# Transposing DMAs for one more chunk's mixer and mlp rows, with a new schedule table

## The chip, the cores and the metric

The kernel runs on one core of a Trainium2 chip. The core has five engines, each with its own queue of instructions: PE (TensorE, matmuls and, beside them, the loading of weights), ACT (ScalarE), DVE (VectorE), POOL (GpSimd) and SP (SyncE, which here only issues DMAs). They meet through semaphores. The metric is the device time of one execution in microseconds (us); less is better.

## The reference

Two layers, each an attention and a mixer with an mlp, over 2048 rows of 512 elements in bf16. All four residual additions take place on the same x.

```python
def _A_ref(x, wq, wk, wv, wo):              # 32 query heads of 16, one key and value head
    q = (x @ wq).reshape(B, S, H, Dh).transpose(0, 2, 1, 3)
    k = x @ wk
    v = x @ wv
    p = softmax(einsum("bhqd,bkd->bhqk", q, k) * Dh ** -0.5)
    return einsum("bhqk,bkd->bhqd", p, v).transpose(0, 2, 1, 3).reshape(B, S, H * Dh) @ wo

def _B_ref(x, w1, w2, w3, w4):
    h = gelu(layernorm(x) @ w1)
    # four quarters of the columns, shifted by +1, -1, +2, -2 rows, zeros at the ends
    hs = concatenate([g0, g1, g2, g3], axis=-1) @ w2
    x1 = x + hs
    return x1 + gelu(layernorm(x1) @ w3) @ w4    # w3: 512 x 1792

for _ in range(2):
    x = x + _A_ref(layernorm(x), A_wq, A_wk, A_wv, A_wo)
    x = x + _B_ref(layernorm(x), B_w1, B_w2, B_w3, B_w4)
```

The attention has 2 x 32 x 2048 x 2048 scores, each of which needs an exponential.

## The kernel before

**Tiles and chunks.** The 2048 rows are 16 tiles of 128. A chunk is the group of query tiles that attention handles together: four chunks of four tiles in the first layer; in the second four, four, four, two and two (`CHUNKS`). So "the second layer's third chunk" is tiles 8 to 11, in the code `la == 1` and `c == 2`.

**Attention.** For each chunk, eight blocks of four heads, each over 16 blocks of keys. PE makes scores into PSUM (`qk`, line 1256). A half of a block's scores is then turned into exponentials in one of two ways. ACT does it with its exp function, 128 x 1024 at a time (`declare_unit`, line 1299, tile EA). Or DVE makes an approximation from integer arithmetic on the bits of a bf16 number, 128 x 512 at a time (`declare_pair`, line 1319, tile J), and two shifted copies of J follow (`shift_op`, line 1356), on POOL or DVE, whichever the planner finds freer; a shift takes one or two rows of 1024. PE multiplies both kinds by the values (`declare_pv`, line 1411; with EA and VP, or with J and VD) into an accumulator, which DVE copies out (line 1460).

**Normalising.** An accumulator goes to DRAM and back by SP (lines 1467 and 1469), its sums too (1551 to 1561). For the last blocks PE does it (lines 1528, 1579, 1594).

**After a chunk's attention** (`chunk_end`). Per tile the output projection (`outproj`, lines 815 and 1724), then the mixer (`mixer_in`, `mix`) and the mlp (`mlp`, `mlp_out`). Line 815 is that of the helper `dot`, which issues most matmuls in groups of four. `mixer_in` takes statistics (950, 952, 972, 970 and others), normalises into Y (987), and POOL normalises once more into ZR (1738). `mlp` normalises Y into ZR on DVE (987). ZR has four slots, and tile `tb` uses slot `tb % 4`, in both. The rows must then be transposed into ZT, so that PE can contract over the columns; this happens in one of two ways, which is what the change is about:

- `across`: PE transposes against an identity matrix, 16 small matmuls a tile (line 1034), into PSUM, and DVE copies two tiles at a time from there to ZT (line 1043).
- `ship`: SP issues one transposing DMA a tile, from ZR to ZT (line 1049); PE, PSUM and DVE have no part in it.

`shipped` (line 1052) chooses by layer and chunk. For the mlp the chunk is that of the group's first tile. The mlp of a chunk works on the tiles that have all their neighbours (`ripe`), so it runs one tile behind: in the second layer tiles 0 to 2, 3 to 6, 7 to 10, then 11 and 12, then 13 to 15.

W1's products go to GP (line 1768, or by ACT with gelu at 1764 in the last chunk), gelu runs over them (1777), two columns at the edges are copied between chunks by POOL (1788, 1790), and `mix` multiplies by W2. The mlp's 14 column blocks are cast to G (line 1864), gelu runs over a tile of G at a time (line 1879), and `mlp_out` multiplies by W4 and adds to X (1898). W3 comes in seven loads through three slots (RING). A change of function on ACT between exp and gelu needs a table load, which the profile lists as ACT_TABLE_LOAD.

**What sets the order.** `Plan` is a list scheduler that runs when the kernel is built. It keeps a heap of ready operations per engine, and its own model of durations, and writes out a fixed order for each engine. It decides there too which halves of the scores go to DVE (`assign`), and which engine shifts; and it puts in filler matmuls (`filler`, IDENT by NIL) where it expects PE to be idle too long. So the number of exponentials on ACT is an outcome of the planning. `TEMPER` is a string with one digit per 5 us of planned time (`STRETCH`); `temper` takes the digit as an index into `MOODS`, sets of limits by which the planner chooses. Any change of it, or of one operation, can move all later ones.

Of the kernel before, what the change touches and what calls it, by code (L numbers as in the profile page):

```python
# [661 lines left out]
class Kernel:  # L662
# [54 lines left out]
    )  # L717
    TEMPER = (
        "2280110c0c4d0a5404a77cda3cec04ccc043cb888a8e7685c67a47d737a46d1da4c7c8087cb1e28da695756a5c"
        "cc5401146a1d88c663f0b1a828a71d6771b4777604c30177000144c8400603ca66525013c2ad97e6e0064640a8"  # L720
        "bc0140560764745d734a7cdaddd3a20b49aa7716ba6d7772a777054b4aac3cb0217daf153ba686b0b548c6cc20"
        "1d522133002012000"
    )

    def __init__(self, nc, ins, out):
# [325 lines left out]

    def shipped(self, kind, la, c):
        last = c == len(self.CHUNKS[la]) - 1
        return c<=1

    def ln_in(self, la, tiles, prio=None):

# [882 lines left out]
```

## Time and profile before

| | |
|---|---|
| median of 3 runs | 1440.35 us (1439.69 to 1441.27) |
| the profiled execution's own time | 1442.68 us |
| its span, from first to last instruction | 1440.8 us |
| mean granted TensorE clock | 0.996 |
| transposing DMAs into ZT | 38, of 46 in all |
| their issue on SP | 1.25 us median |
| issue to landing | 2.4 / 2.5 / 4.4 us (least, median, most) |
| casts from PSUM to ZT (line 1043) | 16, of 0.41 to 0.69 us |
| first exponential begins, last ends | 13.5 us, 1376.6 us |

The profile is of one execution, and its times run from the start of the span. Of a group of instructions it gives the line in the kernel, the engine, the tiles written and read, the shapes and the count, then the busy time, the mean time of one in ns, and the engine's idle time before them with what ended it. PE's busy time is modelled, as matmuls are pipelined. The chain that ended last is followed back from the last instruction, step by step, to what released each.

### The profile page before, as it was taken

The page shows a single profiled execution, that of the slowest core. Times are in us where ns is not written, and L with a number is a line of the kernel's source. Part 1 is how long each engine was busy: PE and PEld are TensorE (multiplying, and loading weights), DVE is VectorE, ACT ScalarE, POOL GpSimd, SP SyncE. Part 2 cuts the span into 40 slices and gives each one's busy share as a digit, 9 for nine tenths or more (in the row PEclk, how much of TensorE's full clock was granted, in tenths as well). Part 3 has the DMA queues.
Part 4 walks back from the last instruction along what each step waited for, and adds up shares of the span by engine and source line. Part 5 has one row for each costly group of instructions (what it writes and reads, how often), then busy time and mean ns, then how long its engine had stood idle before and what let it go on. Part 6 is the DMA issues. An engine that isn't in the chain of part 4 may idle for free.

```text
span 1440.8 us, 61689 instructions
## 1 busy us (share of the span) xinstructions
PE 1415.1 (98%) x27972; PEld 624.6 (43%) x27972; DVE 1311.7 (91%) x2348; ACT 1374.1 (95%) x1463; POOL 1143.0 (79%) x807
## 2 busy tenths in 40 slices
PE   8999999999999999999999999999999999999999
PEld 4344334443433444444344434434434335545575
DVE  8999999999999998998988899999999999978863
ACT  7999999999999999999989999999999999999952
POOL 2888999888889888897855498888889888878831
PEclk9999999999999999999999999999999999999999
DMA  5200121101221011211011011320021111113122
GB/s 156 38 13 17 32 64 43 45 19 37 54 45 49 18 28 45 54 46 36 20 54 32 17 32 29 83 60 23 18 61 39 49 35 46 33 48 78 41 76 59
DMA packets 124335, 63.97 MB, mean 44 GB/s; under 512 B 43945, under 2 KB 124073, under 8 KB 124073
## 3 DMA queue, kind: packets, MB, share of 16 engines
q1 hardware_dynamic: 124072, 60.03, 16.4%
q8 instruction: 219, 3.59, 1.0%
q14 instruction: 44, 0.35, 0.1%
HBM read 40.14 MB, written 10.29 MB: 35 GB/s over the span
## 4 chain that ended last, share of the span: by engine, by line
ACT 63%; PE 18%; DVE 9%; POOL 7%; DMA 1%; issue 1%; SPq 0%; POOLq 0%
ACT EA L1299 59%; PE PB L815 7%; DVE J L1319 6%; POOL J L1356 5%; PE PB L1256 5%; PE PB L1411 5%; ACT G L1879 2%; DVE J L1356 1%; ACT GP L1777 1%; ACT L1299 1%; DVE ST L950 1%; POOL SM L970 1%; ACT L1777 1%; POOL ZR L1738 0%; DMA ad_dram<-ACCF 0%
## 5 line engine op out<-in xcount | busy, mean ns | idle before, releaser
L1299 ACT ACTIVATE EA<-PB 128x1024 bf16<-128x1024 f32 x1381 | 1271.3, 1145 | 16.0 <-PE PB L1256 15.2
L1356 POOL TENSOR_SCALAR J<-J 128x2048 uint16<-128x2048 uint16 (+1 forms) x538 | 992.0, 1844 | 192.4 <-DVE J L1319 83.9
L1319 DVE TENSOR_SCALAR J<-PB 128x512 uint16<-128x512 f32 x1334 | 848.2, 680 | 48.7 <-PE PB L1256 44.0
L1256 PE MATMUL PB<-QT,KT 32*128 32x512 bf16 (+1 forms) x4608 | 590.2, 361 | 8.6 <-ACT EA L1299 3.3
L1411 PE MATMUL PB<-J,VD 128*32 128x256 bf16 (+1 forms) x8964 | 421.1, 265 | 3.8 <-POOL J L1356 1.9
L1411 PE MATMUL PB<-EA,VP 128*32 128x256 bf16 (+1 forms) x6228 | 335.4, 265 | 4.0 <-ACT EA L1299 1.1
L1256 PEld LDWEIGHTS PB<-QT,KT 32*128 32x128 bf16 x4608 | 160.5, 91 | 382.6 <-ACT EA L1299 287.0
L1411 PEld LDWEIGHTS PB<-J,VD 128*32 128x32 bf16 x8964 | 188.8, 96 | 164.5 <-issue 111.0
L1411 PEld LDWEIGHTS PB<-EA,VP 128*32 128x32 bf16 x6228 | 143.9, 96 | 128.6 <-issue 106.6
L815 PE MATMUL PB<-ZT,RING 128*32 128x512 bf16 (+2 forms) x2112 | 128.5, 339 | 0.1
L1356 DVE TENSOR_SCALAR J<-J 128x2048 uint16<-128x2048 uint16 (+1 forms) x165 | 118.5, 719 | 10.4 <-POOL J L1356 8.1
L815 PE MATMUL PB<-W,G 128*32 128x512 bf16 x1624 | 106.2, 381 | 1.0 <-ACT G L1879 1.0
L1864 DVE CAST G<-PB 128x512 bf16<-128x512 f32 (+2 forms) x126 | 71.7, 577 | 12.0 <-PE PB L815 11.6
L970 POOL TENSOR_TENSOR SM<-SM,MH 128x2 f32<-128x2 f32 (+1 forms) x69 | 52.7, 765 | 21.8 <-DVE SM L972 11.2
L815 PEld LDWEIGHTS PB<-W,G 128*32 128x32 bf16 x1624 | 41.4, 96 | 38.1 <-issue 17.2
L815 PEld LDWEIGHTS PB<-ZT,RING 128*32 128x32 bf16 x2112 | 46.0, 96 | 27.0 <-issue 22.0
L1879 ACT ACTIVATE G<-G 128x1792 bf16<-128x1792 bf16 x29 | 46.9, 1683 | 9.8 <-DVE G L1864 9.7
L1898 DVE TENSOR_TENSOR X<-PB,X 128x512 bf16<-128x512 f32 x32 | 21.9, 686 | 30.5 <-PE PB L815 30.0
L1842 POOL TENSOR_TENSOR X<-Y,X 128x512 bf16<-128x512 bf16 x32 | 38.9, 1225 | 11.4 <-DVE Y L1820 8.6
L950 DVE BATCH_NORM_STATS2 ST<-X 128x6 f32<-128x512 bf16 x64 | 43.1, 683 | 2.4 <-DMA X<-in_A_x_dram 1.9
L1460 DVE CAST ACCF<-PB 128x512 bf16<-128x512 f32 (+1 forms) x65 | 40.0, 616 | 0.8 <-PE PB L1411 0.5
L815 PE MATMUL PB<-ZT,W 128*32 128x512 bf16 (+1 forms) x576 | 38.9, 358 | 0.3 <-issue 0.3
(110 smaller groups left out, 682.0 us busy)
## 6 DMA issues: line engine op xcount, KB each, us to landing
RING<-in_B_w_dram SPq DMA_DIRECT2D x66, 256.0 KB, 2.9
ad_dram<-ACCF SPq DMA_DIRECT2D x54, 128.0 KB, 1.8
WO<-in_A_wo_dram SPq DMA_DIRECT2D x9, 512.0 KB, 3.8
WO<-in_B_w_dram SPq DMA_DIRECT2D x9, 512.0 KB, 4.7
OT<-ad_dram SPq DMA_DIRECT2D x108, 32.0 KB
OZ<-rd_dram SPq DMA_DIRECT2D x21, 128.0 KB
X<-in_A_x_dram SPq DMA_DIRECT2D x8, 256.0 KB, 4.8
QT<-QS SPq DMA_DIRECT2D x32, 64.0 KB, 2.4
```

The costliest lines, as they stand in the source:

```text
L815: ins = e.matmul(self.PB[32 * g:32 * g + 32, bank, 0:n], lhsT=lhsT[:, 32 * g:32 * g + 32], rhs=rhs, start=start, stop=stop, tile_position= ...
L950: op("DVE", lambda e, tb=tb: e.bn_stats(self.ST6[:, tb, :], src(tb)), reads=[tagf(tb)], writes=[("ST", tb)], dur=0.606, prio=prio)
L970: op("POOL", lambda e: e.tensor_tensor(out=out, in0=src, in1=self.MH[:, 0, a:b], op=ALU.pow), reads=tags + [("MH",)], writes=tg(r), dur=0. ...
L1256: ins = e.matmul(self.PB[:, bank, j * n:(j + 1) * n], lhsT=self.KT[32 * h:32 * h + 32, la, (kb + j) * 128:(kb + j + 1) * 128], rhs=self.QT ...
L1299: o = q.feeds = op("ACT", lambda e: e.activation(self.EA[:, ea, :, :], self.PB[:, L.bank[0]:L.bank[0] + 2, :], ACTF.Exp, scale=0.25), writ ...
L1319: o = op("DVE", lambda e, i=i, L=L: e.tensor_scalar(out=self.J[:, 3 * s, i * 512:(i + 1) * 512], in0=self.PB[:, L.bank, :], scalar1=128 * ...
L1356: o = self.pl.op(eng, lambda e: e.tensor_scalar(out=self.J[:, d, :], in0=self.J[:, f, :], scalar1=float(self.STEP), scalar2=1.0, op0=ALU.a ...
L1411: ins = e.matmul(self.PB[32 * x:32 * x + 32, A.bank, p * hw:p * hw + hw], lhsT=v[:, la, kb + j, :], rhs=ap[:, i, j * w + u * hw:j * w + u ...
L1460: self.last_copy = op("DVE", lambda e: e.tensor_copy(acc, self.PB[:, A.bank, 0:n]), writes=[ac] + am, dur=t_ps(n), prio=0, side=False, give=A)
L1842: op("POOL", lambda e, tb=tb: e.tensor_tensor(out=self.X[:, tb, :], in0=self.Y[:, tb % 6, :], in1=self.X[:, tb, :], op=ALU.add), reads=[(" ...
L1864: op("DVE", lambda e, f=f, L=L: e.tensor_copy(self.G2[:, f, 0:n], self.PB[:, L.bank, 0:n]), writes=[L] + [(x, f, i) for x in ("G2", "GE") ...
L1879: self.pl.op("ACT", lambda e, i=i: e.activation(self.G2[:, :, i * 128:(i + 1) * 128], self.G2[:, :, i * 128:(i + 1) * 128], ACTF.Gelu_appr ...
```

## The change

`shipped` returns true also for the third chunk of the second layer. That takes in the mixer's rows of tiles 8 to 11, and the mlp's rows of tiles 11 and 12, whose group begins in that chunk: six tiles. (The mlp's group 7 to 10 begins in the second chunk, and its rows were transposed by DMA before too.) The rows for the queries, keys and values (`ln_in`) pass a layer of 0 to the function, so nothing changes for them. `TEMPER` is replaced by another string of the same length, 287 digits, 250 of which differ. As the planner sees other operations and other limits, the whole order is new from the first microseconds on.

```diff
     TEMPER = (
-        "2280110c0c4d0a5404a77cda3cec04ccc043cb888a8e7685c67a47d737a46d1da4c7c8087cb1e28da695756a5c"
-        "cc5401146a1d88c663f0b1a828a71d6771b4777604c30177000144c8400603ca66525013c2ad97e6e0064640a8"
-        "bc0140560764745d734a7cdaddd3a20b49aa7716ba6d7772a777054b4aac3cb0217daf153ba686b0b548c6cc20"
-        "1d522133002012000"
+        "028606a8707aa0a4a077377c7cac7ae13ac54718897680e0973c0a03a3e7e776fcc0220817730020c6cca60782"
+        "775e7d7e7cacd88876a516237797007a4a75c2c7c57521686ec0c005c0020101725002060c7dc72040e07c21b1"
+        "8146c0055672aaaa739ea77bcdcbc228747c710108554c776c0cde367ac00a8866607027567605621a20517472"
+        "0bd80203022000203"
     )
...
     def shipped(self, kind, la, c):
         last = c == len(self.CHUNKS[la]) - 1
-        return c<=1
+        return c<=1 or la and c<=2
```

## The prediction

> **What bounds the kernel now.** I read the page's busy shares, its chain that ended last, and its costliest groups, in that order.
>
> ```profile
> PE 1415.1 (98%) x27972; PEld 624.6 (43%) x27972; DVE 1311.7 (91%) x2348; ACT 1374.1 (95%) x1463; POOL 1143.0 (79%) x807
> ...
> ACT 63%; PE 18%; DVE 9%; POOL 7%; DMA 1%; issue 1%; SPq 0%; POOLq 0%
> ...
> L1299 ACT ACTIVATE EA<-PB 128x1024 bf16<-128x1024 f32 x1381 | 1271.3, 1145 | 16.0 <-PE PB L1256 15.2
> ```
>
> ACT carries the chain: 1381 exponentials at 1271.3/1381 = 0.921 us each, idle only 16.0 us before them. PE's 98% is modelled matmul ends and says little. So I asked the timeline of ACT where its idle time lies, and the windows for the clock in the two other gaps.
>
> ```profile
> 728.04 17.52 ACT L1299 ACTIVATE EA<-PB 128x1024 bf16<-128x1024 f32 x19
> 751.02 9.27 ACT L1299 ACTIVATE EA<-PB 128x1024 bf16<-128x1024 f32 x10 [5.46 <-PE PB L1256]
> 760.31 1.28 ACT L1879 ACT_TABLE_LOAD   x1
> 761.61 4.87 ACT L1879 ACTIVATE G<-G 128x1792 bf16<-128x1792 bf16 x3
> ...
> 1376.59 1.28 ACT L1777 ACT_TABLE_LOAD   x1
> 1378.82 1.06 ACT L1777 ACTIVATE GP<-GP 128x1024 bf16<-128x1024 bf16 x1 [0.94 <-DVE G L1864]
> ...
> 415.00:420.00 5.00, 5.00 (x67) 1.61 (x64) 4.20 (x8) 3.53 (x4) 4.83 (x3) 0.67 0.25 30
> ...
> 1300.00:1305.00 5.00, 5.00 (x130) 3.34 (x130) 3.44 (x8) 3.71 (x4) 3.13 (x3) 0.50 0.59 47
> ```
>
> (In a windows line the busy times are PE, PEld, DVE, ACT, POOL, then the granted clock.) The reader is to see three things. At the layer boundary ACT stands 5.46 us for keys of layer 1. The clock dipped twice, to 0.67 and 0.50, and by the timeline ACT lost 2.35 us (415 to 418) and 2.25 us (1297 to 1305) about them. And the last exponential ends at 1376.6, so 64.2 us of the 1440.8 are a tail in which exponentials count for nothing. There I followed the chain, and the timeline of POOL:
>
> ```profile
> 1382.08 14.55 PE PB L815 x269
> 1396.63 0.41 PE PB L1034 x23
> ...
> 1397.31 0.71 POOL ZR L1738
> 1398.01 0.04 issue
> 1398.06 0.63 PE PB L1034 x32
> 1398.69 2.94 PE PB L815 x106
> ...
> 1397.31 0.70 POOL L1738 TENSOR_SCALAR ZR<-Y,SM 128x512 bf16<-128x512 bf16 x1 [1.75 <-PE PB L1034]
> ```
>
> PE is dense to 1396.6. Then it transposes the mlp rows of tiles 11 and 12, which lay ready since 1387.6 (the line 987 pair at 1386.89). POOL can't write row slot 3 for tile 15 before tile 11 has left it: it waits 1.75 us, and only then come the mixer transposes of tiles 14 and 15.
>
> **What the change does to the counts.** By the order in which both programs' instructions stand as built (it holds no times), after has 1378 exponentials for 1381, 1340 DVE halves (line 1319) for 1334, 576 transposing matmuls from ZR for 672, 3 fewer casts to ZT (line 1043), 12 fewer filler matmuls and 6 more transposing DMAs. Shift rows go from POOL to DVE: POOL 1033 to 1019, DVE 301 to 321. The six DMAs are four mixer tiles (8 to 11) and two mlp tiles: the mlp group 7 to 10 was shipped already, since its first tile belongs to the second chunk. All else that differs is the planner's new order.
>
> **Part 1, the work on ACT.** 3 x 0.921 = 2.76 us less, on the path. This is firm, as every exponential of both programs stands ahead of the tail. It is paid by DVE: +6 halves x 0.636 (848.2/1334) = 3.8, shifts +16 x 0.741 - 12 x 0.614 = +4.5, casts -3 x 0.686 = -2.1; together +6.2 us, hidden in the 129 us in which DVE is not busy. Uncovered, it would cost up to 6.2. POOL gets some 14 us less. **-2.76.**
>
> **Part 2, the layer boundary.** This is new order alone. In before, PE issues no score matmul (line 1256) between 743.9 and 750.6. In after, at the same place (2224 score matmuls done), the gap holds 192 mlp matmuls at 0.042 (4.07/96) = 8.1, 80 transposes at 0.014 (0.45/32) = 1.1, 72 value matmuls at 0.0275 = 2.0, and the key and value projections, 1.0: about 12 us for 6.7. But ACT now has a gelu of three tiles (1.28 + 4.87 + 1.28 us) standing in that gap, after exponential 748, where before it came ten exponentials later. The gelu needs the last of the 14 casts; with PE's order, and DVE's 8.9 us of work beside it, that is 10.6 us after the last score matmul. ACT runs dry 1.7 us after it (743.86 to 745.56 in before) and loads a table for 1.28. Idle: 10.6 - 1.7 - 1.28 = 7.6 for 5.46. Bounds: nothing extra if the casts come 2.1 us sooner; 6 x 0.66 = 4.0 more, so +6.1, if each of the six weight slots costs the 1.96 us that seven loads took in before (13.69/7) instead of PE's 1.30. I take the PE sum, since the slots reload in 1.47 us a piece (three slots, 4.4 us a turn) where PE spends 1.3 and has transposes between. **+2.1.**
>
> **Part 3, the tail.** In after PE's order is: the 224 matmuls up to 1396.6, 32 transposes (tiles 14, 15), 56 mlp matmuls, the 64 of W1. The transposes of tiles 11 and 12, 8 fillers and POOL's wait are gone. Before, W1 ended at 1402.3 and the mix matmuls began at 1403.35; after, in before's times: transposes to 1397.05, cast by 1398.1, 56 x 0.028 = 1.6 to 1398.65, W1 1.9 to 1400.5, gelu and POOL's edge copy 0.7 beside 56 more mlp matmuls, mix at 1402.1: **-1.25**. And the last mlp matmuls of the earlier group now stand ahead of the last exponential's value matmuls, so that the 0.94 us wait on line 1864 and the late line 1528 behind it go: **-1.0**. What is late next is PE itself. The two DMAs issue in 2 x 1.25 us from 1387.7 and land 2.5 us later, by 1392; needed at 1395.3. Behind them on SP wait the W2 load (1389.45, so at most 0.8 later, needed past 1401) and three output stores. Were they late by 4 us, the 1.25 would be lost.
>
> **Part 4, hidden.** Four mixer DMAs near 1235: 5.0 us of SP issue, among the first blocks' round trips through DRAM (lines 1467 to 1561), whose result is read only at 1387. Landing after 2.5 instead of PE 0.63 + DVE 0.69 makes W1 start about 1 to 2 us later; its gelu at 1252.5 has that slack, as its casts lie 4 us apart. 0, at most +1.2. 64 transposes less on PE are 0.9 us beside exponentials: 0, at best -0.9.
>
> **Sum.** -2.76 + 2.1 - 2.25 = -2.9 us. The profiled execution took 1442.68 us with a span of 1440.8 (1.9 around it); the runs' median is 1440.35, and the difference is set on that: **1437.4 us**.
>
> **Rule against row.** DVE's line 987 took 2.09 us at 410.55 instead of 0.4; a POOL shift ran from 410.60 to 412.50, PE then stood 1.15 us, and the clock dropped. The Trainium skill, "SBUF — State Buffer", section "Who interferes with whom", says that such a DVE operation and a GpSimd one contend for one port pair, held for the whole instruction. That agrees with the row and speaks against moving 20 shift rows to DVE, since more meetings mean more such stalls; by it the sum would lie above 1437.4, as in rival B. On the length of the dips the Trainium skill, "TensorE: Matmul & The Clock Gate", section "What's actually happening", gives a free window of about 3.4 us at half clock; the 0.67 and 0.50 over 5 us agree.
>
> **The rivals.** Case A is the sum, with as many dips as before: 1436.2 to 1438.6; 0.35, half of it beyond 0.2% (1437.47). *B, slower:* a new order makes new meetings of line 1356 on DVE and POOL; each that empties PE costs a dip of 2.3 us of ACT. Three more than before's two give 1437.4 + 6.9 = 1444.3; it decides from 2.5 more. For it: 20 more shift rows on DVE; against: only two dips in 1376 us, and 14 fewer rows on POOL. 0.17. *C, fewer dips:* the two were accidents of the old order; one gone gives 1435.1, both 1432.8. 0.27. *D, the boundary costs double, or one or two dips more:* 1439.7 to 1442.0. For it: nothing on ACT covers a gelu that waits. 0.18. *E, the transposing DMAs land late in the tail* (something queued on SP): 1438.7, 0.03; before's 46 landed in 2.4 to 4.4 us, which speaks against.
>
> Within 0.2% (2.9 us, about what a measurement here can tell from no change) are half of A, D and E: 0.38; faster half of A and C: 0.45; slower B: 0.17. The range runs from C with both dips gone to B: 1432.5 to 1444.3.
>
> **What would show it.** Right: ACT idle of 7 to 8.5 us at the boundary, ahead of a three-tile gelu instead of an exponential; last exponential to end 61.5 to 62.5 us; no POOL wait on line 1034 at line 1738 in the tail; the 2.9 us spread over these. Wrong: more than three slices of low clock, or an ACT wait ahead of line 1777 near the third chunk's mixer.

## The result, and the profile after

The changed kernel is **slower**, by 1.1% here: 1457.03 us, the median of four runs (1451.98 to 1461.44), against 1440.81 for the kernel before in the same comparison. The ratio is 1.0110, with a 95% interval of 1.0091 to 1.0128. In two later comparisons, each on one chip, it was 1.0063 (1.0041 to 1.0085) and 1.0072 (1.0056 to 1.0087). The forecast was 1437.4 us, within 1432.5 and 1444.3.

The profiled execution took 1453.54 us, with a span of 1451.6. First the page after: busy shares, the chain's shares, and the group of the exponentials and of the mlp's gelu.

```profile
PE 1415.5 (98%) x27888; PEld 617.1 (43%) x27888; DVE 1318.9 (91%) x2355; ACT 1371.8 (94%) x1460; POOL 1130.3 (78%) x798
...
ACT 56%; PE 31%; DVE 7%; POOL 3%; DMA 2%; issue 1%; POOLq 0%
...
L1299 ACT ACTIVATE EA<-PB 128x1024 bf16<-128x1024 f32 x1378 | 1269.0, 1166 | 21.0 <-PE PB L1256 20.3
...
L1879 ACT ACTIVATE G<-G 128x1792 bf16<-128x1792 bf16 x29 | 46.9, 1683 | 18.4 <-DVE G L1864 18.4
```

The work is what it was said to be: three exponentials fewer, and ACT as busy as before. What grew is the wait for scores (21.0 us for 16.0 ahead of line 1299; of the 16.0 the layer boundary had 5.46, and its wait now stands ahead of line 1879), and PE's share of the chain (31% for 18%). The last exponential ends at 1387.26 for 1376.59; behind it follow 64.3 us for 64.2. So all of the loss lies ahead of the last exponential, and the tail gave nothing. The timeline of ACT says where:

```profile
577.95 1.94 ACT L1299 ACTIVATE EA<-PB 128x1024 bf16<-128x1024 f32 x2 [1.03 <-PE PB L1256]
581.53 1.02 ACT L1299 ACTIVATE EA<-PB 128x1024 bf16<-128x1024 f32 x1 [1.64 <-PE PB L1256]
...
759.20 4.87 ACT L1879 ACTIVATE G<-G 128x1792 bf16<-128x1792 bf16 x3 [7.83 <-DVE G L1864]
...
1245.35 1.02 ACT L1299 ACTIVATE EA<-PB 128x1024 bf16<-128x1024 f32 x1 [1.89 <-PE PB L1256]
...
1308.32 1.94 ACT L1299 ACTIVATE EA<-PB 128x1024 bf16<-128x1024 f32 x2 [1.91 <-PE PB L1256]
...
1387.26 1.28 ACT L1777 ACT_TABLE_LOAD   x1
1390.55 1.06 ACT L1777 ACTIVATE GP<-GP 128x1024 bf16<-128x1024 bf16 x1 [2.01 <-DVE G L1864]
```

Beside the boundary's 7.83 us and the 2.01 us behind the last exponential these are three places, and each begins with a wait and goes on with smaller ones: 1.03 + 1.64 + 0.70 + 0.49 + 0.49 = 4.35 us from 577 to 586; 1.89 + 0.52 + 0.49 = 2.90 from 1243 to 1248; 1.91 + 0.23 + 0.49 + 0.70 + 0.50 + 0.49 = 4.32 from 1306 to 1317. Together they are 11.6 us; the kernel before lost 2.35 + 2.25 = 4.6 us in its two such places. The smaller waits fall into stretches of low clock, 20.5 us in all ahead of the tail for 10.2 in before, as the windows show (busy times of PE, PEld, DVE, ACT, POOL, then the granted clock):

```profile
575.00:580.00 5.00, 3.28 (x45) 1.02 (x41) 4.99 (x6) 3.86 (x5) 2.76 (x2) 0.96 0.13 26
580.00:585.00 5.00, 5.00 (x60) 1.71 (x64) 3.56 (x6) 2.28 (x3) 1.90 (x1) 0.50 0.14 29
...
1245.00:1250.00 5.00, 5.00 (x112) 2.24 (x110) 3.43 (x6) 3.64 (x4) 1.75 (x1) 0.66 0.09 23
...
1310.00:1315.00 5.00, 5.00 (x66) 1.54 (x58) 2.85 (x5) 3.33 (x4) 2.99 (x4) 0.50 0.59 164
```

Ahead of each stands a stall of PE. Here are the timelines of DVE, POOL and PE about the first, of DVE and PE about the third, and of POOL, SP's queue and PE about the second:

```profile
573.91 2.09 DVE L987 TENSOR_SCALAR QS<-X,MV,SM 128x512 bf16<-128x512 bf16 x1
577.12 1.68 DVE L987 TENSOR_SCALAR QS<-X,MV,SM 128x512 bf16<-128x512 bf16 x1
...
573.96 1.90 POOL L1356 TENSOR_SCALAR J<-J 128x2048 uint16<-128x2048 uint16 x1
576.75 1.90 POOL L1356 TENSOR_SCALAR J<-J 128x2048 uint16<-128x2048 uint16 x1 [0.90 <-DVE J L1319]
...
576.65 0.39 PE L1256 MATMUL PB<-QT,KT 32*128 32x512 bf16 x1 [1.05 <-DVE J L1319]
579.45 0.53 PE L1256 MATMUL PB<-QT,KT 32*128 32x512 bf16 x1 [0.67 <-DVE J L1319]
...
1303.24 2.09 DVE L987 TENSOR_SCALAR ZR<-Y,MV,SM 128x512 bf16<-128x512 bf16 x1
1305.99 0.72 PE L1256 MATMUL PB<-QT,KT 32*128 32x256 bf16 x4 [0.96 <-DVE J L1319]
...
1236.91 1.90 POOL L1738 TENSOR_SCALAR ZR<-Y,SM 128x512 bf16<-128x512 bf16 x2
...
1239.02 2.58 SPq L1049 DMA_TRANSPOSE ZT<-ZR  x2
...
1244.36 0.61 PE L815 MATMUL PB<-ZT,W 128*32 128x512 bf16 x8 [1.99 <-DMA ZT<-ZR]
1244.90 0.43 PE L1256 MATMUL PB<-QT,KT 32*128 32x256 bf16 x8
```

The first is a meeting, as rival B feared: line 987 and a POOL shift begin 0.05 us apart, line 987 takes 2.09 us instead of 0.4, the half of scores behind it (line 1319) is late, and its PSUM bank with it. The third place (DVE's line 987 at 1303.24, again 2.09 us) is of the same kind. PE stands 1.05 and 0.67 us in the first and 0.96 us in the third. The second is the change itself: the third chunk's last two mixer tiles leave POOL at 1238.81, and W1, the first to read them transposed, starts 5.5 us later. In the kernel before that way led over PE and DVE and took 1.9 us (1236.53 to 1238.40):

```profile
1234.97 1.56 POOL L1738 TENSOR_SCALAR ZR<-Y,SM 128x512 bf16<-128x512 bf16 x2
...
1238.40 0.60 PE L815 MATMUL PB<-ZT,W 128*32 128x512 bf16 x8
```

So there were two suspects, the meetings (theory P) and the transposing DMAs (theory S), and as a third that a new order is worse in many small places (theory O).

### The profile page after: what moved, and what is told of

Read it like the earlier page. It is cut to its first block, busy times and chain, and to the rows that moved or that the text cites. A ratio compares the mean times of both kernels' runs of the same rounds, so it can differ in the third digit from the quotient of the medians.

```text
span 1451.6 us, 61517 instructions
## 1 busy us (share of the span) xinstructions
PE 1415.5 (98%) x27888; PEld 617.1 (43%) x27888; DVE 1318.9 (91%) x2355; ACT 1371.8 (94%) x1460; POOL 1130.3 (78%) x798
## 4 chain that ended last, share of the span: by engine, by line
ACT 56%; PE 31%; DVE 7%; POOL 3%; DMA 2%; issue 1%; POOLq 0%
ACT EA L1299 53%; PE PB L815 11%; PE PB L1256 10%; PE PB L1411 9%; DVE J L1319 4%; POOL J L1356 3%; ACT G L1879 1%; DVE J L1356 1%; ACT GP L1777 1%; DVE ST L950 1%; DMA RING<-in_B_w_dram 1%; ACT L1299 1%; ACT L1777 0%; POOL SM L970 0%; PE PB L1104 0%
## 5 line engine op out<-in xcount | busy, mean ns | idle before, releaser
L1356 POOL TENSOR_SCALAR J<-J 128x2048 uint16<-128x2048 uint16 (+1 forms) x529 | 977.9, 1849 | 211.9 <-DVE J L1319 86.7
L1411 PE MATMUL PB<-J,VD 128*32 128x256 bf16 (+1 forms) x9000 | 425.8, 265 | 7.8 <-DVE J L1319 2.9
L1411 PEld LDWEIGHTS PB<-J,VD 128*32 128x32 bf16 x9000 | 192.1, 96 | 163.0 <-issue 117.9
L815 PEld LDWEIGHTS PB<-W,G 128*32 128x32 bf16 x1624 | 36.6, 96 | 41.3 <-issue 15.9
L1842 POOL TENSOR_TENSOR X<-Y,X 128x512 bf16<-128x512 bf16 x32 | 39.0, 1227 | 11.6 <-DVE Y L1820 10.1
```

What stands on the lines that cost most here:

```text
L815: ins = e.matmul(self.PB[32 * g:32 * g + 32, bank, 0:n], lhsT=lhsT[:, 32 * g:32 * g + 32], rhs=rhs, start=start, stop=stop, tile_position= ...
L1356: o = self.pl.op(eng, lambda e: e.tensor_scalar(out=self.J[:, d, :], in0=self.J[:, f, :], scalar1=float(self.STEP), scalar2=1.0, op0=ALU.a ...
L1411: ins = e.matmul(self.PB[32 * x:32 * x + 32, A.bank, p * hw:p * hw + hw], lhsT=v[:, la, kb + j, :], rhs=ap[:, i, j * w + u * hw:j * w + u ...
L1842: op("POOL", lambda e, tb=tb: e.tensor_tensor(out=self.X[:, tb, :], in0=self.Y[:, tb % 6, :], in1=self.X[:, tb, :], op=ALU.add), reads=[(" ...
```

## The experiments

### Waits that keep POOL out of DVE's way

The planner has a rule for long POOL operations that it starts within 0.4 us after a DVE operation that it marks as two-port: they wait for the DVE operation *ahead* of that one. So POOL is let go just when line 987 begins. Here they wait for the operation itself. Only waits change; the order of every engine is as it was. The edit touches 69 POOL operations in the changed kernel and 75 in the one before.

```diff
-                o.preds.add(self.order["DVE"][-2])
+                o.preds.add(x)
```

For the changed kernel:

> The changed kernel in its own order; only waits differ: a long POOL operation that the planner starts within 0.4 us after a two-port DVE operation waits for that operation itself, where before it waited for the one ahead of it. Theory P (meetings of line 987 on DVE with a POOL shift, line 1356, empty PE and cost clock dips): the 2.09 us rows at 573.9 and 1303.2 shrink to 0.4 us, the 4.35 us of ACT gaps at 577 to 586 and the 4.32 us at 1306 to 1317 go, and 1457.0 falls by 8.7 to about 1448. Theory S (the transposing DMAs themselves are the cost, at W1 of the third chunk and in the tail): 1457 stays. Theory O (neither; a new order is simply worse in many small places): within 2 us of 1457.

Measured: 1448.7 us (1447.7 to 1453.62), ratio to before 1.0056 (1.0037 to 1.0075). Against the 1457.03 us these are the 8.3 us that theory P said. But the changed kernel was not run beside it, and where it ran again (below) it took 1451.66 and 1450.12 us, by which the gain is only 3.0 or 1.4. The profile has no 2.09 us row of line 987 any more, nor gaps at 577 to 586. It has no wait at W1 either (0.04 us), which the edit was not meant to change, so it can't tell P from S. The same edit in the kernel before missed:

> The kernel before with the same edit of waits. Theory P: the 2.09 us row of line 987 at 410.55 shrinks and its dip's 2.35 us of ACT go; 1440.8 falls to about 1438.4. Theories S and O: no change, 1440.8.

Measured: 1447.95 us (1446.54 to 1450.35), 6.8 us *more* than the 1441.14 of the kernel before beside it. Its meeting at 410 is gone, and yet the last exponential comes 3.7 us later: gaps of under 0.3 us on ACT rose from 2.6 to 5.4 us, and the busy time of the exponentials from 1271.3 to 1273.4 us. A new meeting stands at 1300.58 (line 987 took 2.12 us), and PE then waits 1.50 us. Holding up 75 POOL operations costs by itself, so the edit was too wide to measure with.

### W1 without its wait

```diff
-                        ins = self.dot(e, L.bank, n, self.W1[:, dc, f * 128:(f + 1) * 128], ZT[:, dc, 0:n],
-                                       dc == 0, dc == 3)
+                        ins = self.dot(e, L.bank, n, self.W1[:, dc, f * 128:(f + 1) * 128],
+                                       (self.W1 if (la, c) == (1, 2) else ZT)[:, dc, 0:n], dc == 0, dc == 3)
...
-                if p.eng == "PE" and o.eng == "PE":
+                if p.eng == "PE" and o.eng == "PE" or p.dma and o.free:
...
-                   take=L if h == 0 else None)
+                   take=L if h == 0 else None).free = (la, c) == (1, 2)
```

> The changed kernel in its own order; the W1 matmuls of the second layer's third chunk multiply W1 by itself and not by ZT, so they don't wait for the transposing DMAs; that chunk's mixer result is left out of the computation. Theory S as the main cause: the 1.99 us wait, the dip behind it and what follows from them go, and most of the 16 us comes back, 1447 or less. Theory P: only the 1.89 + 0.52 + 0.49 = 2.9 us of ACT gaps at 1243 to 1248 go, about 1454. Theory O: no change, 1457.

Measured: 1447.82 us (1442.94 to 1451.57), ratio 1.0044 (1.0029 to 1.0059). Against 1457.03 us it came out between the theories; against the 1451.66 and 1450.12 us of the later runs the gain is 3.8 or 2.3. The gaps at 1243 to 1248 are gone; the meetings at 574 and 577 are still there. The third meeting, at 1303, did not take place in this profile, though the edit does nothing about it. With the wide edit of waits on top:

> Both edits in the changed kernel's order (the third chunk's mixer result is left out). If the two causes are independent the gains add: 8.7 + 2.9 = 11.6 us, about 1445.4. Theory S alone: as with the W1 edit alone. Theory O: within 2 us of 1457.

Measured: 1448.57 us (1444.98 to 1452.76), no better than either alone. This fits none of the three; the price of the wide edit, seen in the kernel before, is the likely reason, and the narrow one below bears that out.

### Table and rule, crossed

Only one of the two parts of the change in each. The planner's orders are the same up to the third chunk's mixer of the second layer, and part there.

```diff
# the table of before, the new rule
-        return c<=1
+        return c<=1 or la and c<=2
...
# the new table, the rule of before
-        return c<=1 or la and c<=2
+        return c<=1
```

> The table of before with the new rule for shipping: its order is that of before up to the third chunk's mixer of the second layer, some 90% of it, and it has 1386 exponentials for before's 1381. Theory P/O (the new order of the rest is what costs): 1441.1 + 5 x 0.92 = 1445.7 for the exponentials, plus up to 2.9 if its W1 too waits for the transposing DMAs: 1445 to 1449. Theory S (the shipping is the cost): like the changed kernel, 1453 or more.

Measured: 1449.65 us (1446.69 to 1450.96), ratio 1.0049 (1.0034 to 1.0064).

> The new table with the old rule for shipping: its order is that of the changed kernel up to the third chunk's mixer of the second layer; it has 1385 exponentials for 1378. Theory P/O: what is lost ahead of 1235 us (4.35 + 1.13 of ACT gaps at 577 to 625, 2.4 more at the layer boundary) stays, and 7 x 0.92 = 6.4 us of exponentials come on top, less the 2.9 at W1: 1457.0 + 6.4 - 2.9 = 1460, and in any case above 1452. Theory S: near before with 4 exponentials more, 1441.1 + 3.7 = 1444.8.

Measured: 1452.89 us (1450.63 to 1453.48), ratio 1.0071 (1.0056 to 1.0086). On the same chip the changed kernel:

> The changed kernel once more, unedited, on the chip of the next three, as their reference. If its clock dips are fixed by its order, its runs show a granted clock of 0.986 to 0.993 again and 1452 to 1461 us; if they belonged to one chip or one moment, it comes nearer to 1445.

Measured: 1451.66 us (1445.77 to 1457.73), mean clock 0.989 to 0.996. So neither part is the cause by itself: the new rule alone costs 7.4 us on the old table (1442.25 before, in this comparison), the old rule on the new table 10.6, both 9.4. The first of them has no wait at W1 at all; five exponentials more (4.6 us) and a longer wait behind the last one (5.66 us for 0.94) do the harm there:

```profile
1388.05 1.06 ACT L1777 ACTIVATE GP<-GP 128x1024 bf16<-128x1024 bf16 x1 [5.66 <-DVE G L1864]
```

What a rule for the DMAs does to the time is thus, in these two orders, mostly what the planner makes of it afterwards.

### Only the meetings, and both causes

The narrow edit: only where the DVE operation is line 987 and POOL's a shift (15 operations in the changed kernel).

```diff
-                o.preds.add(self.order["DVE"][-2])
+                o.preds.add(x if (x.emit.__code__.co_firstlineno, o.emit.__code__.co_firstlineno) == (987, 1356) else self.order["DVE"][-2])
```

> The changed kernel in its own order; of the waits edited in the first run here only 15 remain: a POOL shift (line 1356) that the planner starts within 0.4 us after line 987 on DVE waits for that operation's end. If the meetings of these two are the cause, this keeps the whole gain of the wider edit (8.3 us, to 1448.7) and, since it holds POOL up less, gains up to some us more: 1443 to 1449. If the gain of the wider edit came from other pairs, it stays near 1457.

Measured: 1448.6 us (1445.94 to 1453.82), ratio 1.0059 (1.004 to 1.0077): the meetings named are gone from the profile (ACT runs from 559.21 for 41.36 us without a gap), and W1's wait is still there (2.03 us). Against the changed kernel beside it the gain is 3.1 us and not 8.3. Its runs spread over 7.9 us, those of the changed kernel over 12.0. In the kernel before it does nothing, so it has no price of its own:

> The kernel before with the narrow edit of waits (25 here), whose wide form made it 6.8 us slower. If the price of the wide edit came from the other pairs: 1440 to 1442, unchanged, or some tenths less. If holding a POOL shift behind line 987 costs by itself: 1444 to 1448, and the gains of the edit in the changed kernel are understated by as much.

Measured: 1440.96 us (1439.5 to 1442.54), ratio 0.9998 (0.999 to 1.0007). Then the narrow edit with W1 by W1:

> Both named causes taken out of the changed kernel's order, the narrow edit of 15 waits for the meetings and W1 by W1 for the wait on the transposing DMAs (the third chunk's mixer result is left out). Theory that the two are the loss: ACT gaps of 4.35, 4.32 and 2.9 us go together and the granted clock rises to 0.998 or more; 1452 to 1457 falls by 8 to 12, to about 1444. Theory that something else in the new order holds the time: no lower than either edit alone, 1448.

Measured: **1442.12 us** (1440.07 to 1447.16), ratio 1.0012 (1.0002 to 1.0023). The page and ACT's timeline of this kernel:

```profile
PE 1407.9 (98%) x27888; PEld 623.3 (43%) x27888; DVE 1315.6 (91%) x2355; ACT 1371.0 (95%) x1460; POOL 1130.5 (79%) x798
...
L1299 ACT ACTIVATE EA<-PB 128x1024 bf16<-128x1024 f32 x1378 | 1268.2, 1150 | 9.4 <-PE PB L1256 8.4
```

```profile
559.78 54.22 ACT L1299 ACTIVATE EA<-PB 128x1024 bf16<-128x1024 f32 x59
...
1235.57 14.92 ACT L1299 ACTIVATE EA<-PB 128x1024 bf16<-128x1024 f32 x16
```

The wait for scores is 9.4 us for 21.0; ACT runs through 577 to 586 and 1243 to 1248 without a gap. The exponentials and their order are those of the changed kernel. To have the shares apart, all four corners on one chip:

> The changed kernel again, unedited, as the corner of a two by two on one chip. 1450 to 1458, mean clock 0.987 to 0.996, with the meetings at 574, 577 and 1303 and a W1 wait of 1.7 to 2.0 us in its profile.

> The narrow edit of waits alone. If the two causes add: the corner less about 6 us. If the clock's dips need both (one stall preparing the next), little less than the corner.

> W1 by W1 alone (the third chunk's mixer result is left out). If the two causes add: the corner less about 4 to 6 us, of which 2.9 are the ACT gaps and the rest dips; the meetings stay in its profile.

> Both (the third chunk's mixer result is left out). 1442 again, a clock of 0.999 or more in most runs; if the causes add, the gain is the sum of the two single gains within 2 us.

| on one chip (before: 1441.05) | median us | ratio to before, 95% |
|---|---|---|
| changed kernel | 1450.12 | 1.0072 (1.0056 to 1.0087) |
| without the meetings | 1445.79 | 1.0027 (1.0011 to 1.0043) |
| without W1's wait | 1446.12 | 1.0038 (1.0026 to 1.0050) |
| without both | 1441.83 | 1.0010 (0.9999 to 1.0021) |

By the medians the two add: 4.3 and 4.0 us alone, 8.3 together, of 9.1 to be explained. Each edit gains, and both together bring most of it back: none of their intervals reaches the 1.0056 at which that of the changed kernel begins. But each interval is about 2 us wide to either side, so the halves, and that they add, are known to some 3 us only. With that, theory O falls for most of the loss, and P and S each hold for about half.

Neither cause is in every execution. In the profile of W1 by W1 alone the meetings at 574 and 577 did not take place, though they were expected and nothing ahead of W1 differs; nor did they with the new table and the old rule. In that of both edits one did, at 243.91 (2.13 us), which the narrow edit didn't keep apart. As to W1's wait: in the profile without the meetings PE reached W1 at 1242.04, 4.0 us after SP began to issue the last pair of transposing DMAs, and found them landed; in that of the wide edit it came after 3.8 us and waited 0.04. In the four others that transpose these rows by DMA in this order PE was there 3.4 to 3.7 us after the issue and waited 1.68 to 2.03 us, so the rows came 5.3 to 5.7 us after it. So the DMAs' landing varies by more than 1 us too.

### The price of a stall, by hand

```diff
+    def extra(self, e, src):
+        k, at = next(self.nth), (43, 59, 70, 77)
+        for i, n in enumerate((512, 512, 256) if k in at else ()):
+            e.bn_stats(self.SCR[:, 3 * at.index(k) + i, :], src[:, 0:n])
...
-        self.pl.op("DVE", lambda e: e.tensor_scalar(
+        self.pl.op("DVE", lambda e: [self.extra(e, src), e.tensor_scalar(
```

> The kernel before in its own order, with DVE held up four times by 1.7 us (three bn_stats into a tile that nothing reads, ahead of a line 987 instruction, at 585, 770, 951 and 1135 us): what one meeting of DVE with a POOL shift does to DVE, put in by hand. If each costs ACT the 2.3 us that the prediction reckoned: 1441.5 + 9.2 = 1450.7. If each costs 4.3 us, as the rows at 577 and 1306 of the changed kernel have it: 1458. If PE mostly has other work in hand and a hold-up of DVE is no cause by itself: 1441 to 1444.

Measured: 1446.33 us (1444.58 to 1451.46), 5.3 us more than the 1441.02 beside it, or 1.3 for each. That is below the 2.3 of the prediction and far below the 4.3 of the changed kernel. The last of the four, by the timelines of DVE, PE and ACT and the windows:

```profile
1137.43 1.60 DVE L1909 BATCH_NORM_STATS2 SCR<-Y 128x6 f32<-128x512 bf16 x3
...
1140.89 0.39 PE L1256 MATMUL PB<-QT,KT 32*128 32x512 bf16 x2 [1.75 <-DVE J L1319]
...
1142.19 1.94 ACT L1299 ACTIVATE EA<-PB 128x1024 bf16<-128x1024 f32 x2 [1.74 <-PE PB L1256]
```

```profile
1140.00:1142.00 2.00, 1.11 (x21) 0.53 (x21) 2.00 (x5) 0.45 (x1) 0.48 (x1) 1.00 0.33 66
1142.00:1144.00 2.00, 2.00 (x46) 1.03 (x47) 2.00 (x4) 1.81 (x2) 1.84 (x2) 1.00 0.42 72
```

PE stood 1.75 us, ACT lost 1.74, and the clock stayed at 1.00, so nothing followed. The same profile also repeats the very stall of the kernel before at 414: there PE waits 1.15 us (for line 1319) in both, ACT loses 1.06 here, and 1.19 + 0.50 + 0.66 in the profile of before, where the clock dropped. The windows of before, and of this kernel:

```profile
414.00:416.00 2.00, 2.00 (x37) 0.88 (x35) 2.00 (x5) 0.81 (x2) 1.49 (x1) 0.72 0.32 66
416.00:418.00 2.00, 2.00 (x26) 0.49 (x18) 1.67 (x3) 1.37 (x2) 1.92 (x2) 0.50 0.59 63
```

```profile
414.00:416.00 2.00, 1.89 (x40) 0.96 (x40) 2.00 (x5) 0.94 (x2) 1.27 (x1) 1.00 0.36 74
416.00:418.00 2.00, 2.00 (x29) 0.55 (x26) 2.00 (x5) 2.00 (x3) 1.92 (x2) 1.00 0.42 66
```

Behind the four hold-ups PE waited 1.31, 0.88, 1.06 and 1.75 us, and ACT lost 1.32, 0.69, 0.47 and 1.74. So a stall of PE cost ACT about its own length or less, and the dip is a second price that comes with some stalls only.

### W1 planned later

```diff
-                self.ship(part, zdst, [[t] for t in ztag])
+                self.ship(part, zdst, [[t] for t in ztag], size=600000 if (la, c) == (1, 2) else 400000)
```

> The changed kernel with the narrow edit of waits, and with the planner told 600000 bytes for 400000 for the four mixer transposing DMAs of the third chunk, so that it plans W1 later (last landing 5.6 us behind the first issue; the trace had 5.3); nothing is left out, and the order is that of the changed kernel up to that W1; 1379 exponentials. If the early W1 and the meetings are the loss: no wait on ZT over 0.5 us and 1444 to 1446. If something else in the order: 1448 or more.

Measured: 1446.97 us (1445.97 to 1452.37), ratio 1.0049 (1.0035 to 1.0064). The wait at W1 is gone (ACT runs from 1229.43 for 31.43 us without a gap), and the gain of it is given back at the end, where 67.9 us follow the last exponential for 64.3, much as with the old table:

```profile
1384.22 1.06 ACT L1777 ACTIVATE GP<-GP 128x1024 bf16<-128x1024 bf16 x1 [6.17 <-DVE G L1864]
```

The likely reason, which no run shows, is that the later W1 has set back what follows it on PE, up to the last mlp columns. No version here beats the kernel before.

## Why the prediction was wrong

**The base.** The sum was made on a profile with two dips, and case A kept "as many dips as before". But of the 76 runs of before that stand beside the experiments 72 have a mean clock of 0.999 or 1.000; the profiled execution, with 0.996, was one of the rare ones. The changed kernel shows 0.986 to 0.996 in all its 16 runs. Over these, a straight line gives 1443.0 us at full clock and 1.36 us more for each thousandth of clock lost (correlation -0.95). That line is argued, not shown, but it says the same as the corners: without stalls and dips the new order is worth about as much as the old.

**Rival B was right in kind, and got too small a chance.** It was given 0.17, and three more dips, 6.9 us together. The meetings of line 987 with the shift cost 4.3 us on one chip, about half of what there was to lose. Its reason did not hold: it counted 20 more shift rows on DVE, but of DVE's shifts 11 took over 1 us in after and 14 in before. What met POOL's shift was line 987, as in the row at 410. The profile of after had ten rows of line 987 over 0.9 us where before had six; three of them emptied PE. "Against: only two dips in 1376 us" counted one execution as if it were the rule.

**Part 4, "hidden, 0, at most +1.2", is the step that failed.** It cost 4.0 us by the medians above. The delay was under-sized: the DMAs brought W1 5.5 us behind the rows and not "about 1 to 2 us later" than before's 1.9, as two issues of 1.3 us stand one behind the other and the rows of the second came 4.0 us after its own issue (1240.3 to 1244.36). And the cover named for it was the wrong one: the slack of W1's gelu at 1252. (The casts ahead of that gelu lay 4.6, 2.1 and 4.4 us apart in before, and not 4 throughout.) The waiting matmul stands in PE's own queue, with eight score matmuls right behind it (1244.90 in the profile), and ACT has about 1.1 us of scores in hand: PE stops at 1242.37, ACT at 1243.46. What was queued behind the waiting instruction was not asked, and the sign of being wrong looked for the wait ahead of line 1777, where it came ahead of line 1299.

**Part 3, the tail, failed too.** It forecast -2.25 and got nothing (64.3 us for 64.2). Its first half was right in kind: POOL's wait and the two tiles' transposes are gone, but PE then waits 0.76 us for a load of W3, so the way from the end of the earlier group's W4 matmuls (1408.57; 1396.63 in before) to the mix matmuls took 6.0 us for 6.7, a gain of 0.7 and not 1.25. Its second half turned round. The 0.94 us wait on line 1864 did not go but grew to 2.01, as PE stood ahead of the earlier group's last mlp matmuls:

```profile
1389.16 0.61 PE L815 MATMUL PB<-ZT,RING 128*32 128x512 bf16 x8 [1.24 <-issue]
...
1414.15 0.62 PE L815 MATMUL PB<-ZT,RING 128*32 128x256 bf16 x16 [0.76 <-DMA RING<-in_B_w_dram]
```

The wait comes back in the kernel without both causes (1.01 us, and 1.99 on ACT), so it belongs to this order. What PE waits for there the profile doesn't name, and no run settles it.

**Parts 1 and 2 were right.** Three exponentials fewer are in the page. The boundary took 7.83 us where 7.6 was forecast, and 7.6 to 8.1 in all other profiles with the new table, ahead of the three-tile gelu as said. A wait of 0.71 us behind that gelu (at 768.02), which before has not, was left out of the sum.

**What is left.** By parts 1 and 2 the kernel without both causes should be 0.3 to 0.7 us below before; measured it is 0.8 above (interval -0.1 to 3.0). A part is a third kind of stall, which neither edit touches. In 12 of the 13 profiles with this table DVE stands 1.2 to 2.0 us between 612 and 623 for a DMA of the round trip through DRAM (line 1556 or 1564), with score halves queued behind; in the same twelve ACT then loses 1.1 to 5.7 us up to 632, and in eight of them a low clock follows. In the thirteenth DVE doesn't wait there, and ACT has no gap. With the old table DVE waits 1.1 us at most there, and ACT loses 0.8 at most. Here it is in the changed kernel's second profile, on DVE and ACT:

```profile
614.29 0.35 DVE L1556 RECIPROCAL ZS<-ZS 128x32 bf16<-128x32 bf16 x1 [1.88 <-DMA ZS<-ad_dram]
...
617.13 1.94 ACT L1299 ACTIVATE EA<-PB 128x1024 bf16<-128x1024 f32 x2 [1.32 <-PE PB L1256]
```

No run took this wait out, so its price is open; with the dip behind it ACT lost 5.66 us in this profile. A gap of 1.4 us at 1322 in the kernel without both causes stays unexplained.

**The rule on the shared port.** What the Trainium skill says in "SBUF — State Buffer", section "Who interferes with whom", was set against the sum, and spoke for the right side: by it the time was to lie above 1437.4. The corners agree, with 4.3 us. The Trainium skill, "TensorE: Matmul & The Clock Gate", section "What's actually happening", also says that the clock's window of 3413 ns runs freely and doesn't reset with the kernel. The traces agree: by the clock's records in the traces, in each of the twelve profiles with more than one low stretch these begin whole multiples of 3.413 us apart (in after at 579.56, 1245.16 and 1306.60, which is 195 and 18 windows) and, but for the one that some have at the end of the span, last whole multiples of it (2, 1 and 3 windows).

## What to carry to other kernels

Before an operation is called hidden, look at what stands behind its reader in the reader's own queue, and at how much the bounding engine has in hand: here a 2 us wait of PE, for products whose gelu came 16 us later, reached ACT within 1.1 us, as PE works in order. One profile of the kernel before is one draw: when its clock and those of its other runs differ, a forecast by the profile's dips forecasts noise, and stalls of PE should be counted and priced instead, at their own length (1.3 us here for a 1.7 us hold-up of DVE) and with a chance of a dip on top. And where a list scheduler rewrites the order, test each part of a change on both tables before crediting or blaming it.

## What the runs showed of the hardware that was not expected

- The same stall may or may not cost a dip. PE's wait of 1.15 us at 414 brought half clock for 3.4 us in one profile and none in another; a wait of 1.75 us brought none, one of 0.96 (at 1306 in after) brought 10.2 us. Where the stall falls on the grid above doesn't settle it: in before the wait (412.74 to 413.89) lay inside the window from 411.48 to 414.89 and a dip followed; with the old table and the new rule the same wait (413.21 to 414.36) lay inside the window from 412.83 to 416.24 and none did, and PE was busy for 2.26 of the 3.41 us in both. But the odds go by how busy PE is in a window. Between 100 and 1376 us of the 16 profiles with a low stretch, a window at full clock in which PE was busy (by its modelled records) for under 62% was followed by a low one in 11 cases of 11; at 62 to 80% in 15 of 67, at 80 to 90% in 3 of 220, and above that in none of 5618. No run moved a stall against the grid.
- Of two that meet, the one that begins first need not be the one that runs. At 573.91 DVE's line 987 began 0.05 us ahead of POOL's shift and took 2.09 us, while the shift took its usual 1.90. Where the shift waited for line 987 itself, this meeting was gone; with the wait for the operation ahead of it, as the planner has it, the two begin together.
- The way over transposing DMAs is longer than the one over PE and DVE, and its length varies more. Issue to landing was 2.4 to 4.6 us in after, with 1.25 us of SP's queue for each at the median, where PE and DVE needed 0.67 and 0.69 us for two tiles in before.
